# Load order, queues and input transposes at the start of a long-convolution kernel with a two-row router

## The chip, the cores and the metric

The kernel runs on one core of a Trainium2 chip. The core has TensorE (matrix products, into PSUM), VectorE, ScalarE, GpSimd and SyncE, each with its own strictly ordered list of instructions; they meet through semaphores. Transfers are started from an engine's list (here SyncE's and ScalarE's) and carried out by 16 DMA engines. The metric is the device time of one execution in microseconds (us); less is better.

## The reference, cut to what matters

```python
x = A_u                                           # (1, 2048, 512) bf16
g = sigmoid((x * gate_w).sum(-1, keepdims=True))  # a gate for each row
a = A_ref(x, ...)     # a long convolution along the rows, one kernel K for each of 512 channels:
                      #   dt = exp(log_dt); P = exp(dt*(A_re + 1j*A_im) * l)    for 2048 lags l
                      #   K  = real(sum_n C * P * dt*B)                          n = 128 states
                      #   a  = irfft(rfft(x) * rfft(K)) + x * Dskip
b = B_ref(B_x, ...)   # r = x @ w_r; the two rows with the largest r go through
                      #   silu(x_sel @ w_gate) * (x_sel @ w_up) @ w_down, times sigmoid(r),
                      #   and are added to x at their places
return g * a + (1 - g) * b
```

The kernel takes its rows, and those of the second branch, from the one input A_u.

## The kernel before, in words

**Data.** U holds the 2048 x 512 input in SBUF: 16 row blocks of 128 rows, arranged so that within each 256 rows the even and the odd ones are apart. XT holds the input transposed (512 channels on partitions, in four groups of 128). PRM holds the six parameter tables (A_re, A_im, C_re, C_im, B_re, B_im), each 512 x 128 in memory and 128 x 512 in SBUF, so each is transposed by the DMA that loads it. LDT is log_dt spread over all partitions. F is the 2 MB matrix of the forward transform; NG, two buffers, is a part of its negative, loaded in four pieces. CB and CF hold constants (the identity among them), WL the two weight vectors of gate and router. WG, WU and WD are the weights of the two-row feed-forward.

**Stages.** (1) Parameters: DTB = exp(LDT), AL = DTB * A_re, B16 = the phase step from DTB * A_im, WW from B and C. (2) For each half h of the channels, tables of exp(AL * lag) (`exps1`, `exps2`: 32 and 16 activations) times sines and cosines of B16 * lag (`trig`, called by `tab1` and `tab2`). (3) `routing`: logits of gate and router (`lg`, 64 products of XT with WL), two rounds of a maximum over all rows (`gmax`: VectorE reduces, TensorE transposes, VectorE reduces, twice a round), gathering the two rows, the feed-forward (`ffn1` for gate and up, Silu, `dn`), and one-hot rows OHR to put the result back. (4) `forward`: the transform of the input, 16 blocks of 16 matmuls (two more in the second half of the rows), each block evicted from PSUM to X. (5) `xupd`: the branch's rows are added to U, and U is scaled by 1 - g. (6) `kgen` and `kspec`: the convolution kernel and its transform for each half, from the tables and a 3.5 MB matrix KP. (7) `products` and `inverse` for each half, and the stores.

**Order.** Each operation is put into a list by `P.op` with an engine, what it reads and writes, an estimated cost and a priority. `schedule()` then plays a model of the engines and queues: it places, again and again, the operation that can start earliest in the model, and among equals the one with the longest way to the end plus its priority. `P.boost = 100` stands while `routing()` is written down. That play fixes the order on each engine; at run time each engine goes through its list and waits by semaphores. `EV` gives an eviction to ScalarE or VectorE, whichever would be done first in the model; `SCL` does the same for the angle operations. DMA issues are placed in the same way: those with `eng=SP` on SyncE's list, those with `eng=ACT` on ScalarE's. `tset` numbers the phases of ScalarE's function tables (exponential in even, sine, tanh and Silu in odd): no operation of a later phase is placed before all of an earlier one are. Phase 0 is `exps1(0)` and `exps2(0)`; 1 is `tab1(0)`, half of `tab2(0)` and the router's tanh and Silu; 2 is `exps1(1)`; 3 the rest of `tab2(0)` and `tab1(1)`; 4 is `exps2(1)`; 5 is `tab2(1)`.

**The loads at the start.** On SyncE's list: LDT; the transposing loads of A_re and A_im; four transposing loads of A_u into XT, one for each 128 channels; the transposing loads of C_re, C_im, B_re and B_im; CF, WG, WU, two pieces of NG, Dskip. On ScalarE's list: the two halves of U, F, CB, and the two loads of WL.

`lg` reads XT by rows in U's even and odd order, so with a step of two:

```python
last = h.matmul(b(0, 128, tb * 2, (1, 2)),
                XT(0, 128, db * L + 1024 * j + 256 * st + par, (2, 128)),
                WL(0, 128, db * 2, (1, 2)), start=(db == 0), stop=(db == 3))
```

In the profile the helpers `TT`, `TS`, `AC`, `EV`, `SCL`, `CP`, `STT` and `DMA` record their operations under their own lines: L387 is a VectorE operation on two tensors (`TT`), L391 and L392 one with a scalar (`TS`), L394 `STT`, L396 `CP`, L398 an activation (`AC`), L402 an eviction (`EV`), L406 an angle operation (`SCL`), L409 a load or store. L242 is a table load of ScalarE, L463 and L475 the transposing loads of parameters and input, L598 `lg`, L612 a reduction and L617 a transpose of `gmax`, L639 the gather, L648 the one-hot transposes, L659 `ffn1`, L670 `dn`, L693 and L695 `forward`, L713 to L732 `kgen`, L754 `kspec`, L804 `inverse`, L830 and L831 `xupd`.

Of the kernel before, what the change touches and what calls it, by code (L numbers as in the profile page):

```python
# [27 lines left out]
def dr(a, off, *dims):  # L28
    return bass.AP(a.tensor, off, [[s, c] for (s, c) in dims])
# [225 lines left out]
L, D, NS, NF = 2048, 512, 128, 1792  # L255
# [71 lines left out]
def bass_gated_mix__ssm_conv_s4__moe_arch_mod__prompt_kernel(nc, A_u, A_A_re, A_A_im, A_B_re, A_B_im, A_C_re, A_C_im, A_log_dt, A_Dskip,  # L327
# [24 lines left out]
    with ExitStack() as es:  # L352
# [55 lines left out]
        def DMA(pairs, rd, wr, nbytes, eng=SP, **k):  # L408
            return P.op(eng, lambda h: [h.dma_start(o, i) for o, i in pairs], rd, wr, cost=0.5 * len(pairs), n=len(pairs), nbytes=nbytes, dma=True, **k)  # L409
# [42 lines left out]
        def misc(bf=False):  # L452
            mc[0] += 1
            return (misb if bf else mis)[mc[0] % 2]
# [6 lines left out]
        DMA([(LDT(0, 128, 0, (1, D)), dr(A_log_dt, 0, (0, 128), (1, D)))], [], [LDT], 131072, prio=2e5)  # L461
        for i in (1, 0, 2, 3, 4, 5):
            P.op(SP, lambda h, i=i: h.dma_start_transpose(PRM(0, 128, i * D, (1, D)), dr(prm[i], 0, (128, D), (1, 128))), [], [(PRM, i)], cost=1.25, nbytes=131072, prio=(1.9e5 if i < 2 else 1.2e5) - 1e3 * i)  # L463
        for j in range(2):
            DMA([(U(0, 128, j * 8 * D, (2 * D, 4), (1, 2 * D)), dr(A_u, 1024 * j * D, (2 * D, 128), (256 * D, 4), (1, 2 * D)))], [], [(U, t) for t in range(8 * j, 8 * j + 8)], 1048576, eng=ACT, prio=2e5)
        DMA([(F(0, 128, 0, (1, 8192)), f_c[:, :])], [], [F], 2097152, eng=ACT, prio=1.9e5)
        DMA([(CB(0, 128, 0, (1, 384)), cb_c[:, :])], [], [CB], 98304, eng=ACT, prio=1.8e5)
        def ld_w(h):
            with nc.allow_non_contiguous_dma(reason="tiny weight vectors"):
                a = h.dma_start(WL(0, 128, 0, (2, 4), (1, 1)), dr(gate_w, 0, (1, 128), (128, 4), (1, 1)))  # L470
                b = h.dma_start(WL(0, 128, 1, (2, 4), (1, 1)), dr(B_w_r, 0, (1, 128), (128, 4), (1, 1)))
            return [a, b]
        P.op(ACT, ld_w, [], [WL], cost=1.0, n=2, nbytes=100000, dma=True, prio=1.7e5)
        for db in range(4):
            P.op(SP, lambda h, db=db: h.dma_start_transpose(XT(0, 128, db * L, (1, L)), dr(A_u, db * 128, (D, L), (1, 128))), [], [(XT, db)], cost=4.2, nbytes=524288, prio=1.5e5)  # L475
        DMA([(CF(0, 128, 0, (1, 160)), cf_c[:, :])], [], [CF], 81920, prio=1.1e5)
        DMA([(WG(0, 128, 0, (NF, 4), (1, NF)), dr(B_w_gate, 0, (NF, 128), (128 * NF, 4), (1, NF)))], [], [WG], 1835008, prio=1.0e5)
        DMA([(WU(0, 128, 0, (NF, 4), (1, NF)), dr(B_w_up, 0, (NF, 128), (128 * NF, 4), (1, NF)))], [], [WU], 1835008, prio=0.9e5)
        DMA([(DSK(0, 1, 0, (1, D)), dr(A_Dskip, 0, (D, 1), (1, D)))], [], [DSK], 1024)

        IDN = lambda *a: CB(0, 128, *a)

# [104 lines left out]


        def routing():
            b = misc()  # L590
            def lg(h):
                last = None
                for j in range(2):
                    for st in range(4):
                        for par in range(2):
                            tb = j * 8 + st * 2 + par
                            for db in range(4):
                                last = h.matmul(b(0, 128, tb * 2, (1, 2)), XT(0, 128, db * L + 1024 * j + 256 * st + par, (2, 128)), WL(0, 128, db * 2, (1, 2)), start=(db == 0), stop=(db == 3))  # L598
# [78 lines left out]
        def forward():  # L677
            np_ = [0]
            for ft in range(4):
                ng = NG[ft % 2]  # L680
                DMA([(ng(0, 128, 0, (128, 8), (1, 128)), bass.AP(fn_c.tensor, fn_c.offset + ft * 128, [[4096, 128], [512, 8], [1, 128]]))], [], [ng], 262144)
# [225 lines left out]
```

## Time and profile before

| | us |
|---|---|
| median of three runs | 247.95 (247.47 to 248.18) |
| the profiled execution | 246.49 |
| its span, first to last instruction | 244.7 |
| TensorE busy in it | 172.5 (70%) |
| VectorE busy in it | 170.4 (70%) |
| ScalarE busy in it | 146.9 (60%) |

The busy times are those of one profiled execution. The page cuts the span into 40 slices and gives the busy share of each engine in each slice as a digit (9 is 90% or more); the timeline lists instructions by their start, with the wait before them and what ended it in square brackets; a line that begins with SPq or ACTq is the issue of a transfer on that engine's list. TensorE's matmuls overlap, so that its busy time is not its time at full rate. The mean granted TensorE clock over the span was 0.927 of full speed.

### The profile page before, as it was taken

How to read it: one execution, taken by the hardware profiler on the slowest of the kernel's cores; microseconds unless marked ns; L12 is line 12 of the kernel's file. 1: busy time of each engine (PE TensorE's matmuls, PEld its weight loads, DVE VectorE, ACT ScalarE, POOL GpSimd, SP SyncE). 2: the span in 40 equal slices, each digit the busy share in tenths (PEclk: the TensorE clock that was granted, in tenths of full speed). 3: DMA queues.
4: the chain of work that ended last, by engine and by line, in shares of the span. 5: the costliest groups of instructions: out<-in, count | busy, mean ns of one | idle time of the engine just before them, and what ended most of it. 6: DMA issues, size and time to landing. Idle time of an engine off the chain costs nothing.

```text
span 244.7 us, 3534 instructions
## 1 busy us (share of the span) xinstructions
PE 172.5 (70%) x1426; PEld 103.4 (42%) x1426; DVE 170.4 (70%) x279; ACT 146.9 (60%) x278; POOL 0.2 (0%) x4
## 2 busy tenths in 40 slices
PE   0000030349999999999899506999898999973993
PEld 0000020147444444445555201366665667862882
DVE  0002223899995039989850299969999999999872
ACT  0330999349989899549876999656664454404000
POOL 0000000000000000000000000000000000000000
PEclk9999999999999999999999755589997999996798
DMA  4999959903600101000006800000027000001144
GB/s 143 324 253 161 205 120 360 330 3 87 217 0 3 43 0 43 3 0 0 4 0 220 378 5 0 1 0 3 0 46 300 3 0 0 3 0 48 38 132 128
DMA packets 25953, 22.03 MB, mean 90 GB/s; under 512 B 17233, under 2 KB 23506, under 8 KB 25554
## 3 DMA queue, kind: packets, MB, share of 16 engines
q1 hardware_dynamic: 23538, 17.52, 25.9%
q10 hardware_dynamic: 2400, 4.30, 6.7%
q8 instruction: 11, 0.18, 0.3%
q14 instruction: 4, 0.03, 0.0%
HBM read 16.83 MB, written 2.10 MB: 77 GB/s over the span
## 4 chain that ended last, share of the span: by engine, by line
PE 43%; DVE 24%; ACT 20%; DMA 8%; issue 3%; SPq 1%; DVEq 0%; ACTq 0%
DVE AR L387 21%; PE ps L693 19%; ACT AR L398 13%; DMA AR<-in_A_A_im_dram 8%; PE ps L804 7%; PE ps L754 6%; ACT AR L402 3%; PE ps L831 3%; PE ps L830 2%; ACT AR L406 2%; DVE AR L391 2%; PE ps L659 1%; PE ps L670 1%; PE ps L695 1%; ACT L242 1%
## 5 line engine op out<-in xcount | busy, mean ns | idle before, releaser
L387 DVE TENSOR_TENSOR AR<-AR 128x1024 bf16<-128x1024 bf16 (+5 forms) x182 | 136.8, 804 | 34.7 <-DMA AR<-in_A_A_re_dram 11.6
L398 ACT ACTIVATE AR<-AR 128x256 bf16<-128x256 f32 (+2 forms) x132 | 64.7, 560 | 15.4 <-DVE AR L391 4.8
L402 ACT ACTIVATE AR<-ps 128x1024 bf16<-128x1024 f32 (+6 forms) x58 | 45.5, 806 | 30.7 <-PE ps L754 17.7
L693 PE MATMUL ps<-AR 128*128 128x512 bf16 x256 | 59.6, 385 | 0.0
L693 PEld LDWEIGHTS ps<-AR 128*128 128x128 bf16 x256 | 25.1, 99 | 30.5 <-issue 1.9
L804 PE MATMUL ps<-AR 128*128 128x256 bf16 x256 | 30.8, 286 | 5.5 <-ACT AR L398 5.5
L754 PE MATMUL ps<-AR 128*128 128x256 bf16 x224 | 33.3, 286 | 0.7 <-ACT AR L402 0.7
L804 PEld LDWEIGHTS ps<-AR 128*128 128x128 bf16 x256 | 26.1, 103 | 10.0 <-DVE AR L387 5.8
L754 PEld LDWEIGHTS ps<-AR 128*128 128x128 bf16 x224 | 21.9, 101 | 12.2 <-issue 1.5
L398 ACT ACTIVATE AR<-ps,AR 128x512 bf16<-128x512 f32 (+1 forms) x32 | 16.6, 586 | 15.5 <-DVE AR L387 10.4
L598 PE MATMUL ps<-AR 128*128 128x2 bf16 x64 | 1.8, 165 | 32.2 <-DMA AR<-in_A_u_dram 32.2
L406 ACT ACTIVATE AR<-AR 128x256 int32<-128x256 f32 x50 | 17.6, 405 | 10.9 <-DVE AR L387 10.7
L391 DVE TENSOR_SCALAR AR<-AR 128x1024 int32<-128x1024 int32 (+5 forms) x32 | 16.2, 524 | 8.4 <-ACT AR L398 8.0
L402 DVE CAST AR<-ps 128x1024 bf16<-128x1024 f32 (+3 forms) x6 | 5.1, 865 | 22.5 <-PE ps L695 15.4
L830 PE MATMUL ps<-AR 128*128 128x512 bf16 x16 | 8.1, 509 | 11.0 <-ACT AR L398 11.0
L598 PEld LDWEIGHTS ps<-AR 128*128 128x128 bf16 x64 | 1.8, 104 | 32.1 <-issue 32.1
L713 PE MATMUL ps<-AR 128*128 128x84 bf16 x256 | 11.8, 201 | 2.4 <-ACT AR L402 2.4
L713 PEld LDWEIGHTS ps<-AR 128*128 128x128 bf16 x256 | 10.6, 98 | 4.5 <-ACT AR L402 3.2
L617 PE MATMUL ps<-AR 128*128 128x128 f32 x4 | 1.9, 475 | 12.8 <-DVE AR L391 12.8
L394 DVE SCALAR_TENSOR_TENSOR AR<-ps,AR 128x256 bf16<-128x256 f32 x16 | 6.9, 479 | 4.1 <-PE ps L804 4.1
L726 PE MATMUL ps<-AR 128*32 128x128 bf16 (+1 forms) x96 | 8.5, 381 | 0.0
L830 PEld LDWEIGHTS ps<-AR 128*128 128x128 bf16 x16 | 1.6, 100 | 15.7 <-ACT AR L398 14.6
(32 smaller groups left out, 62.1 us busy)
## 6 DMA issues: line engine op xcount, KB each, us to landing
AR<-c_ksp SPq DMA_DIRECT2D x1, 3584.0 KB, 12.5
AR<-in_A_u_dram ACTq DMA_DIRECT2D x2, 1024.0 KB, 12.0
AR<-c_fwd ACTq DMA_DIRECT2D x1, 2048.0 KB, 20.0
AR<-c_inv SPq DMA_DIRECT2D x1, 2048.0 KB, 7.9
out_dram<-AR SPq DMA_DIRECT2D x16, 128.0 KB, 2.2
AR<-in_B_w_gate_dram SPq DMA_DIRECT2D x1, 1792.0 KB, 7.1
AR<-in_B_w_up_dram SPq DMA_DIRECT2D x1, 1792.0 KB, 11.2
AR<-in_B_w_down_dram SPq DMA_DIRECT2D x1, 1792.0 KB, 7.9
```

The costliest lines, as they stand in the source:

```text
L387: return P.op(DVE, lambda h: h.tensor_tensor(out=o, in0=a, in1=b, op=op), rd, wr, cost=tt_cost(o, a, b), **k)
L391: return P.op(DVE, lambda h: h.tensor_scalar(out=o, in0=a, scalar1=s1, scalar2=None, op0=op0), rd, wr, cost=c, **k)
L398: return P.op(ACT, lambda h: h.activation(out=o, in_=a, func=func, scale=scale, bias=bias), rd, wr, cost=0.185 + nel(o) * 0.833e-3 + (0.09 ...
L402: return P.op((ACT, DVE), (lambda h: h.activation(out=o, in_=a, func=ACTF.Copy), lambda h: h.tensor_copy(o, a)), rd, wr, cost=(0.185 + n * ...
L406: return P.op((ACT, DVE), (lambda h: h.activation(out=o, in_=a, func=ACTF.Copy, scale=c), lambda h: h.tensor_scalar(out=o, in0=a, scalar1= ...
L693: last = h.matmul(o, w, U(0, 128, (blk * 8 + st * 2 + par) * D, (1, D)), start=(par + st == 0), stop=(par * 4 + st == 7 and blk == 0))
L713: last = hh.matmul(pb(0, 128, (g - b0) * 84, (1, 84)), TP[h][1 - part](0, 128, g * 128, (1, 128)), TQ[h][1 - part](0, 128, g * 84, (1, 84) ...
L726: last = hh.matmul(pb(32 * g, 32, c4, (256, njg), (4, 64)), lw, KA[h](0, 128, c4 + 4 * (8 * bk + g), (16, njg), (84, 64)), start=True, sto ...
L754: last = hh.matmul(pb(0, 128, n * 256, (1, 256)), KP(0, np_, u * 2048 + tau * 128, (1, 128)), KC[h](0, np_, jg * 256, (1, 256)), start=(k ...
L804: last = hh.matmul(pb(0, 128, e * 256, (1, 256)), G(0, 128, ((par * 2 + part) * 4 + ft) * 512 + (2 * t2 + e) * 128, (1, 128)), X(0, 128, h ...
L830: h.matmul(pb(0, 128, c0, (1, D)), IDN(0, (1, 128)), U(0, 128, tb * D, (1, D)), start=True, stop=False)
L831: return h.matmul(pb(0, 128, c0, (1, D)), OHR(0, 2, tb * 128, (1, 128)), ZB(0, 2, D, (1, D)), start=False, stop=True)
```

## The change

The first loads are put in a fixed order, by falling priorities. LDT, CB and WL go on ScalarE's list, and nothing else. SyncE's list begins with A_re and A_im, then U in two halves, the other four parameter tables, F, CF, two pieces of NG, WG, WU and Dskip. The four transposing loads of A_u are gone; in their place the router begins with eight steps on TensorE, each of which transposes two row blocks of U (eight 128 x 128 transposes into one PSUM buffer), and an eviction of 1024 elements to XT. XT is then in U's order, and `lg` reads it without a step. The first two pieces of NG are no longer loaded from `forward`, and the last two get a higher priority. The planner's estimate of WL's size falls from 100000 to 20000 bytes.

```diff
-        DMA([(LDT(...), dr(A_log_dt, ...))], [], [LDT], 131072, prio=2e5)
-        for i in (1, 0, 2, 3, 4, 5):
-            P.op(SP, lambda h, i=i: h.dma_start_transpose(PRM(0, 128, i * D, (1, D)), dr(prm[i], ...)), [], [(PRM, i)], cost=1.25, nbytes=131072, prio=(1.9e5 if i < 2 else 1.2e5) - 1e3 * i)
-        for j in range(2):
-            DMA([(U(...), dr(A_u, 1024 * j * D, ...))], [], [(U, t) for t in range(8 * j, 8 * j + 8)], 1048576, eng=ACT, prio=2e5)
-        DMA([(F(...), f_c[:, :])], [], [F], 2097152, eng=ACT, prio=1.9e5)
-        DMA([(CB(...), cb_c[:, :])], [], [CB], 98304, eng=ACT, prio=1.8e5)
...
-        P.op(ACT, ld_w, [], [WL], cost=1.0, n=2, nbytes=100000, dma=True, prio=1.7e5)
-        for db in range(4):
-            P.op(SP, lambda h, db=db: h.dma_start_transpose(XT(0, 128, db * L, (1, L)), dr(A_u, db * 128, (D, L), (1, 128))), [], [(XT, db)], cost=4.2, nbytes=524288, prio=1.5e5)
...
+        dp = [3e5]
+        def DQ(pairs, rd, wr, nbytes, **k):
+            dp[0] -= 1e3
+            return DMA(pairs, rd, wr, nbytes, prio=dp[0], **k)
+        def prm_t(i):
+            dp[0] -= 1e3
+            P.op(SP, lambda h: h.dma_start_transpose(PRM(0, 128, i * D, (1, D)), dr(prm[i], ...)), [], [(PRM, i)], cost=1.25, nbytes=131072, prio=dp[0])
+        DQ([(LDT(...), dr(A_log_dt, ...))], [], [LDT], 131072, eng=ACT)
+        DQ([(CB(...), cb_c[:, :])], [], [CB], 98304, eng=ACT)
+        P.op(ACT, ld_w, [], [WL], cost=1.0, n=2, nbytes=20000, dma=True, prio=2.5e5)
+        prm_t(0)
+        prm_t(1)
+        for j in range(2):
+            DQ([(U(...), dr(A_u, 1024 * j * D, ...))], [], [(U, t) for t in range(8 * j, 8 * j + 8)], 1048576)
+        for i in range(2, 6):
+            prm_t(i)
+        DQ([(F(...), f_c[:, :])], [], [F], 2097152)
+        DQ([(CF(...), cf_c[:, :])], [], [CF], 81920)
+        for ft in range(2):
+            DQ([(NG[ft](...), ngsrc(ft))], [], [NG[ft]], 262144)
+        DQ([(WG(...), dr(B_w_gate, ...))], [], [WG], 1835008)
+        DQ([(WU(...), dr(B_w_up, ...))], [], [WU], 1835008)
+        DQ([(DSK(...), dr(A_Dskip, ...))], [], [DSK], 1024)
...
         def routing():
+            for q in range(8):
+                bb = misc(True)
+                def tr(h, q=q, bb=bb):
+                    last = None
+                    for t_ in range(2):
+                        for db in range(4):
+                            last = h.transpose(bb(0, 128, db * 256 + t_ * 128, (1, 128)), U(0, 128, (2 * q + t_) * D + db * 128, (1, 128)), IDN(0, (1, 128)))
+                    return last
+                P.op(PE, tr, [(U, 2 * q), (U, 2 * q + 1), CB], [bb.buf], cost=0.7)
+                EV(XT(0, 128, q * 256, (L, 4), (1, 256)), bb(0, 128, 0, (256, 4), (1, 256)), [bb.buf], [(XT, q)])
...
-                                last = h.matmul(b(...), XT(0, 128, db * L + 1024 * j + 256 * st + par, (2, 128)), WL(...), ...)
+                                last = h.matmul(b(...), XT(0, 128, db * L + tb * 128, (1, 128)), WL(...), ...)
...
-                DMA([(ng(...), ...)], [], [ng], 262144)
+                if ft > 1:
+                    DMA([(ng(...), ngsrc(ft))], [], [ng], 262144, prio=2e5)
```

More of the change, by code (lines that the diff above doesn't have):

```diff
@@ L460, in bass_gated_mix__ssm_conv_s4__moe_arch_mod__prompt_kernel, with ngsrc @@
         prm = [A_A_re, A_A_im, A_C_re, A_C_im, A_B_re, A_B_im]
-        DMA([(LDT(0, 128, 0, (1, D)), dr(A_log_dt, 0, (0, 128), (1, D)))], [], [LDT], 131072, prio=2e5)
-        for i in (1, 0, 2, 3, 4, 5):
-            P.op(SP, lambda h, i=i: h.dma_start_transpose(PRM(0, 128, i * D, (1, D)), dr(prm[i], 0, (128, D), (1, 128))), [], [(PRM, i)], cost=1.25, nbytes=131072, prio=(1.9e5 if i < 2 else 1.2e5) - 1e3 * i)
-        for j in range(2):
-            DMA([(U(0, 128, j * 8 * D, (2 * D, 4), (1, 2 * D)), dr(A_u, 1024 * j * D, (2 * D, 128), (256 * D, 4), (1, 2 * D)))], [], [(U, t) for t in range(8 * j, 8 * j + 8)], 1048576, eng=ACT, prio=2e5)
-        DMA([(F(0, 128, 0, (1, 8192)), f_c[:, :])], [], [F], 2097152, eng=ACT, prio=1.9e5)
-        DMA([(CB(0, 128, 0, (1, 384)), cb_c[:, :])], [], [CB], 98304, eng=ACT, prio=1.8e5)
+        def ngsrc(ft):
+            return bass.AP(fn_c.tensor, fn_c.offset + ft * 128, [[4096, 128], [512, 8], [1, 128]])
         def ld_w(h):
@@ L597, in lg @@
                             for db in range(4):
[L598 removed]
+                                last = h.matmul(b(0, 128, tb * 2, (1, 2)), XT(0, 128, db * L + tb * 128, (1, 128)), WL(0, 128, db * 2, (1, 2)), start=(db == 0), stop=(db == 3))
                 return last
```

16 lines of the change are left out of this document (11 added, 5 removed).

## The prediction, as it stood before the run

> **What bounds the kernel now.** I read the page first: the slices of the span.
>
> ```profile
> span 244.7 us, 3534 instructions
> PE   0000030349999999999899506999898999973993
> DVE  0002223899995039989850299969999999999872
> ACT  0330999349989899549876999656664454404000
> GB/s 143 324 253 161 205 120 360 330 3 87 217 0 3 43 0 43 3 0 0 4 0 220 378 5 0 1 0 3 0 46 300 3 0 0 3 0 48 38 132 128
> ```
>
> A slice is 6.1 us. TensorE does almost nothing for eight slices, ScalarE idles in most of the first four, and VectorE is full only from the seventh on; over the last ten VectorE is full. No engine bounds the whole. So I cut the span where ScalarE changes its function table: exponentials of half 0; sines of half 0 with the router; exponentials of half 1; sines; exponentials; sines; then the products and the last inverse. Windows view (busy time, count in brackets):
>
> ```profile
> 0.00:38.90 38.90, 1.85 (x64) 1.79 (x64) 6.39 (x12) 17.75 (x54) 0.20 (x4) 1.00 1.00 204
> 38.90:72.06 33.16, 21.47 (x249) 12.30 (x250) 29.36 (x69) 24.44 (x42) 0.00 (x0) 1.00 0.50 167
> 72.06:87.97 15.91, 15.91 (x75) 6.97 (x74) 4.58 (x8) 15.04 (x38) 0.00 (x0) 1.00 0.08 18
> 87.97:124.14 36.17, 35.18 (x233) 17.61 (x232) 32.90 (x55) 28.95 (x44) 0.00 (x0) 1.00 0.04 8
> 124.14:138.24 14.10, 13.65 (x126) 6.79 (x124) 3.13 (x5) 10.03 (x24) 0.00 (x0) 0.88 0.53 207
> 138.24:164.77 26.53, 15.93 (x59) 6.65 (x60) 21.87 (x40) 21.41 (x32) 0.00 (x0) 0.61 0.07 29
> 164.77:223.50 58.73, 51.85 (x499) 37.54 (x496) 58.04 (x66) 26.72 (x40) 0.00 (x0) 0.96 0.10 37
> ```
>
> The columns are stretch, length, TensorE, its weight loads, VectorE, ScalarE, GpSimd, clock, DMA share, GB/s. Stage 1 (38.9 us) has 17.75 us of ScalarE work and all 16 DMA engines busy (share 1.00). From stage 2 on ScalarE or VectorE is nearly full, with TensorE beside them. The next views say what stage 1 waits for: ScalarE's timeline, the DMA issues (last number: us from issue to landing), and the queues.
>
> ```profile
> 0.73 1.00 ACTq L409 DMA_DIRECT2D AR<-in_A_u_dram  x2
> 1.76 1.48 ACTq L409 DMA_DIRECT2D AR<-c_fwd  x1
> 6.56 1.28 ACT L398 ACT_TABLE_LOAD   x1 [6.56 <-issue]
> 12.35 1.95 ACT L398 ACTIVATE AR<-AR 128x256 bf16<-128x256 f32 x6 [3.87 <-DVE AR L387]
> 24.99 0.72 ACT L406 ACTIVATE AR<-AR 128x256 int32<-128x256 f32 x2 [10.70 <-DVE AR L387]
> 26.54 12.34 ACT L398 ACTIVATE AR<-AR 128x256 bf16<-128x256 f32 x40
> 38.90 1.28 ACT L242 ACT_TABLE_LOAD   x1
> 66.46 1.00 ACT L402 ACTIVATE AR<-ps 128x1024 bf16<-128x1024 f32 x1
> ```
>
> ```profile
> AR<-in_A_A_re_dram SPq DMA_TRANSPOSE x1, 10.3
> AR<-in_A_A_im_dram SPq DMA_TRANSPOSE x1, 19.4
> AR<-in_A_C_re_dram SPq DMA_TRANSPOSE x1, 2.8
> AR<-in_A_log_dt_dram SPq DMA_DIRECT2D x1, 128.0 KB, 5.0
> AR<-c_bf ACTq DMA_DIRECT2D x1, 96.0 KB, 19.0
> 1.20 1.90 SPq L463 DMA_TRANSPOSE AR<-in_A_A_re_dram  x1
> 4.66 25.11 SPq L475 DMA_TRANSPOSE AR<-in_A_u_dram  x4
> 36.68 7.35 SPq L409 DMA_DIRECT2D AR<-c_fwdn  x2
> ```
>
> The six parameter tables are alike in size; C_re, alone in the queues, lands in 2.8 us, A_re beside the 4 MB of U and F in 10.3, A_im in 19.4. The exponentials need A_re (AL); the angle operations, put on ScalarE after six exponentials, need A_im (B16), and the strict order makes everything behind them wait 10.70 us. The sum is made against the profiled execution, 246.49 us around a span of 244.7; the median of the three runs is 247.95, 1.46 more.
>
> **The change, part by part: stage 1.** ScalarE's queue loses the issues of U and F (1.00 + 1.48 us) and gains that of LDT (A_re's issue at 1.20 follows it, 0.47 after the queues start at 0.73): 6.56 becomes 4.5. Table load 1.28, first exponential 0.63 and VectorE's AL 0.69 follow, so the exponentials start near 7.1 instead of 12.35, if A_re is there: issued at 0.73, it lands at 3.5 with C_re's 2.8, at 11.0 with its own 10.3. I take 2.8, since U is now issued behind it on the same queue and only the small loads run on the other. A_im, issued near 2.7 (A_re's issue took 1.90), lands at 5.5 by C_re's row, 13 by A_re's; B16 comes about 2.4 us of VectorE work later, at 9.4 after AL, or at 15.4. After six exponentials ScalarE is at 9.1: it waits 0.3 us, or 6.3. I take 0.3.
>
> The Trainium skill, page "DMA: Bandwidth & Descriptors", section "Queues, rings and completion order", says that one ring is consumed in order and that each DMA engine takes turns between the queues packet by packet. A_re's 10.3 us beside the other queue's 4 MB agree; by it U on the same ring cannot delay A_re, and the sum would be the one I take.
>
> ScalarE has then 48 exponentials at 12.34/40 = 0.31 (14.8 us), three angle operations at 0.31, and its share of the eight new XT evictions, 1024 elements each, at 1.00 by the row of 66.46: between 0 and 8 of them (VectorE idles here, so 4 is the middle). 7.1 + 14.8 + 0.9 + 4.0 = 26.8 instead of 38.9, **12.1 us** gained; ends 22.8 (16 gained) and, with eight evictions on ScalarE, 30.8 (8 gained), or 37 with A_im late as well.
>
> The 64 TensorE transposes and the reads of U fall into time in which TensorE is idle: eight transposes take 1.01 us below, 8.1 us in all, from about 9 us (U is behind 0.26 MB of transposes; 2.1 MB at 324 GB/s are 6.5 us) to 18. If that cover went, the router would start 8.1 us later, at 26, still ahead of 29.8, when the last input transpose is issued now (4.66 + 25.11). CB, which the transposes need, and WL, which the first logits need, have only LDT ahead of them in their queue: I take LDT's 5.0 us; CB's own 19.0 would put them at 20 to 23, and the router still ahead of 29.8.
>
> What leaves SP's queue are four input transposes, 25.11 us of issue. F goes behind U and four parameter tables: 5.2 MB in all, at the mean of the first five slices (217 GB/s) 24 us, at the best slice (360) 15; I take 22, and NG0 a little later instead of about 44. The gate and up weights come behind them, sooner than now, where they follow all ten transposes. The second NG's issue sat in a full queue for most of 7.35 us; the same stall may now meet it, but behind it wait only DSK, the later NG and the down weights, which nothing needs for 15 us more.
>
> **Stage 2, the sines.** The first forward block needs F and NG0 and ran at 59.4, behind the router's first feed-forward product; it can now run from 23. The views of the chain and of TensorE:
>
> ```profile
> 51.99 1.01 PE L648 MATMUL ps<-AR 128*2 128x128 bf16 x8
> 59.47 10.04 PE ps L693 x40
> 76.82 1.73 PE ps L693 x8
> 78.77 8.63 PE ps L693 x40
> ```
>
> The evictions of forward are what its blocks cost the other engines. A block is two groups of 1.73 us, 3.46 us, and needs one eviction of 1 us. In stage 2 there will be about eight instead of two: six more, three on each engine. Against that, the router's maxima can run under the exponentials, where VectorE idles. Now they stand in VectorE's full stretch:
>
> ```profile
> L391 DVE TENSOR_SCALAR AR<-AR 128x128 f32<-128x128 f32 (+3 forms) x8 | 2.7, 340 | 3.8 <-ACT AR L398 3.6
> L612 DVE TENSOR_REDUCE AR<-ps 128x1 f32<-128x128 f32 x4 | 1.2, 290 | 0.7 <-PE ps L617 0.7
> L394 DVE SCALAR_TENSOR_TENSOR AR<-AR 128x16 f32<-128x16 f32 (+1 forms) x4 | 0.9, 216 | 0.1
> L396 DVE CAST AR<-AR 128x16 f32<-128x16 bf16 (+2 forms) x6 | 0.8, 169 | 0.1
> L612 DVE TENSOR_REDUCE AR<-AR 128x1 f32<-128x16 f32 x4 | 0.7, 170 | 0.1
> ```
>
> That is some 6 us (2.7 less about 1.1 for the tables' own two, then 1.2 + 0.9 + 0.8 + 0.7, and waits of 0.7). VectorE has 29.36 - 6 + 3.6 = 27, ScalarE 24.44 + 3 = 27.5; with a us for waits, stage 2 takes 28.5 instead of 33.16: **4.7 us**. Ends: nothing, where the router stays in the way; 8.7, ScalarE's own 24.44.
>
> **Stages 3 to 5.** Stage 3 is ScalarE's exponentials with forward evictions among them, as now: nothing. In stage 4 VectorE has 32.90 of 36.17; forward, from 23 on, 16 blocks of 3.46 and some 12 us of router between (TensorE's 21.47 us in stage 2 less the 12.6 from 59.47 on, and the down projection), ends near 90 instead of in stage 5, so a few of its evictions leave: **2 us**, ends 0 and 5.3 (down to VectorE's 32.90 less two evictions). In stage 5 ScalarE has 10.03 of 14.10 us:
>
> ```profile
> ACT AR L402 <- PE ps L726: 2.1, 1, 2.1
> ACT AR L398 <- PE ps L695: 1.7, 1, 1.7
> PE ps L830 <- ACT AR L398: 11.0, 2, 10.7
> ```
>
> The first two are waits for TensorE, which does the last forward blocks between the kernel-table products; with forward gone they go: **4 us**, ends 0 and 5.
>
> **Stages 6 to the end.** VectorE has 58.04 of 58.73 us after 164.77, and the stage before takes it 21.87 of 26.53. I take nothing gained; ends are the 4.7 us of that idle time, gained if all of it goes, or lost if it doubles with TensorE's low clock. That was 0.61 in the stage, with a wait of 10.7 us (the last row above). By the Trainium skill, "TensorE: Matmul & The Clock Gate", Part 1, idle windows of about 3.4 us halve the clock and as much activity restores it. The start of forward agrees (the first 40 matmuls took 10.04, the next 40 8.63); the 0.61 over 26.5 us lasts longer than that rule says. By it a shorter wait would give back some of the 4.7 us, and the sum would be up to that much lower, which is part of the good end below; I take the row.
>
> Sum: 12.1 + 4.7 + 2 + 4 = 22.8. 246.49 - 22.8 = 223.7, and 1.46 more for the median: **225 us**.
>
> **The rivals.** *Only the start is kept.* The order of each engine is written by the planner with its own durations; if forward's evictions and the router fill what stage 2 frees, and TensorE still ends forward late, only stage 1's gain counts, with most evictions on ScalarE: 8 to 12 us, 236 to 240. For it speaks that ScalarE is already 74% busy in stage 2; against it, that TensorE's idle first 59 us are real room.
>
> *Slower: the router between forward blocks.* The exponentials of half 1 cannot pass the Silu on ScalarE, and that needs the router's nine TensorE steps (four maxima, gather, two transposes, two products). Now they run with nothing between. With forward ready at 23, each may sit behind a block. At 3.46 us a step Silu comes at 22 + 9 x 3.46 = 53, just inside stage 2's end of 55. If blocks wait in turn for evictions that stand behind sines, a step becomes 7 us: Silu at 85, 13 us after the present 72, less the 6 of stages 4 and 5: 255. It decides from (72 - 22 + 6)/9 = 6.2 us a step. Against it: evictions came every 3.5 us in stage 3 already.
>
> *Everything at its good end:* 16 + 8.7 + 5.3 + 5 + 4.7 = 39.7, so 208.
>
> **How the numbers follow.** The forecast (219 to 234) has 0.53, only the start 0.22, the good end 0.11, slower 0.10, and 0.04 that the pieces cancel within 0.3% (about what three runs can tell). Faster 0.86, same 0.04, slower 0.10. Leaving out the slower rival and the tail of the good end gives 211 to 241.
>
> **What would show it.** Right: A_im lands before 7 us, no wait of ScalarE over 2 us before the second table load, which comes at 23 to 31; no input transposes in SP's queue; the first forward block at 19 to 27; VectorE's maxima before the sines; the third table load near 55. Wrong: parameter tables that still take 10 us, ScalarE waiting for XT's PSUM or for U among the exponentials, Silu after 65, or new waits for TensorE in the sine stages.

## The result

| | median, us | all runs | ratio to before, 95% interval |
|---|---|---|---|
| before, beside the runs of after | 248.06 | 247.47 to 248.38 | |
| after | 225.45 | 224.77 to 227.63 | 0.9106 (0.9039 to 0.9173) |

The change takes 22.6 us off the median; 225 was predicted, 211 to 241 the range. The profiled execution of after took 227.63 us (span 225.8), the slowest of its four runs; its span is 18.9 us below the 244.7 of before, where the prediction's terms add up to 22.8. So 3.9 us of the agreement in the median are not in the trace that is read here: that the median fell on the forecast is in part luck.

### The profile page after: what moved, and what is told of

It is laid out like the page before. It is cut to its first block, busy times and chain, and to the rows that moved or that the text cites. A ratio compares the mean times of both kernels' runs of the same rounds, so it can differ in the third digit from the quotient of the medians.

```text
span 225.8 us, 3655 instructions
## 1 busy us (share of the span) xinstructions
PE 182.8 (81%) x1480; PEld 111.4 (49%) x1490; DVE 173.1 (77%) x283; ACT 151.0 (67%) x282; POOL 0.2 (0%) x4
## 4 chain that ended last, share of the span: by engine, by line
PE 49%; DVE 23%; ACT 21%; issue 3%; DMA 2%; SPq 1%; DVEq 0%; ACTq 0%
DVE AR L387 19%; PE ps L715 18%; ACT AR L398 12%; PE ps L776 8%; PE ps L826 7%; ACT AR L402 6%; PE ps L735 3%; DVE AR L391 3%; PE ps L853 2%; ACT AR L406 2%; PE ps L852 2%; PE ps L748 2%; DMA AR<-in_A_A_im_dram 2%; PE ps L691 1%; PE ps L680 1%
## 5 line engine op out<-in xcount | busy, mean ns | idle before, releaser
L387 DVE TENSOR_TENSOR AR<-AR 128x1024 bf16<-128x1024 bf16 (+6 forms) x182 | 136.9, 804 | 9.3 <-DMA AR<-in_A_A_re_dram 5.8
L402 ACT ACTIVATE AR<-ps 128x1024 bf16<-128x1024 f32 (+7 forms) x62 | 50.2, 827 | 33.9 <-PE ps L776 17.3
L398 ACT ACTIVATE AR<-AR 128x256 bf16<-128x256 f32 (+4 forms) x132 | 65.1, 559 | 3.3 <-DVE AR L387 1.5
L715 PE MATMUL ps<-AR 128*128 128x512 bf16 x248 | 62.9, 408 | 2.0 <-ACT AR L402 1.1
L715 PEld LDWEIGHTS ps<-AR 128*128 128x128 bf16 x256 | 26.4, 104 | 35.5 <-issue 8.6
L826 PEld LDWEIGHTS ps<-AR 128*128 128x128 bf16 x256 | 26.1, 102 | 9.8 <-DVE AR L387 5.7
L776 PEld LDWEIGHTS ps<-AR 128*128 128x128 bf16 x224 | 21.7, 100 | 12.0 <-issue 1.5
L398 ACT ACTIVATE AR<-ps,AR 128x512 bf16<-128x512 f32 (+1 forms) x32 | 16.6, 584 | 15.5 <-DVE AR L387 10.3
L607 PE MATMUL ps<-AR 128*128 128x128 bf16 x64 | 7.5, 311 | 11.6 <-DMA AR<-in_A_u_dram 9.5
L735 PE MATMUL ps<-AR 128*128 128x84 bf16 x256 | 13.3, 214 | 3.2 <-ACT AR L402 3.2
L852 PE MATMUL ps<-AR 128*128 128x512 bf16 x14 | 7.2, 512 | 10.2 <-ACT AR L398 10.2
L735 PEld LDWEIGHTS ps<-AR 128*128 128x128 bf16 x256 | 11.8, 106 | 5.1 <-ACT AR L402 4.3
L607 PEld LDWEIGHTS ps<-AR 128*128 128x128 bf16 x64 | 6.5, 145 | 12.4 <-DMA AR<-in_A_u_dram 9.5
L396 DVE CAST AR<-ps 128x16 bf16<-128x16 f32 (+3 forms) x6 | 1.5, 256 | 13.7 <-PE ps L691 12.9
L402 DVE CAST AR<-ps 128x1024 bf16<-128x1024 f32 (+4 forms) x7 | 5.7, 837 | 7.0 <-PE ps L748 4.4
L852 PEld LDWEIGHTS ps<-AR 128*128 128x128 bf16 x16 | 1.6, 99 | 15.0 <-ACT AR L398 13.1
L853 PE MATMUL ps<-AR 2*128 2x512 bf16 x16 | 7.9, 495 | 0.7 <-DVE AR L402 0.5
## 6 DMA issues: line engine op xcount, KB each, us to landing
AR<-in_B_w_up_dram SPq DMA_DIRECT2D x1, 1792.0 KB, 12.6
```

The source lines that it names most:

```text
L387: return P.op(DVE, lambda h: h.tensor_tensor(out=o, in0=a, in1=b, op=op), rd, wr, cost=tt_cost(o, a, b), **k)
L398: return P.op(ACT, lambda h: h.activation(out=o, in_=a, func=func, scale=scale, bias=bias), rd, wr, cost=0.185 + nel(o) * 0.833e-3 + (0.09 ...
L402: return P.op((ACT, DVE), (lambda h: h.activation(out=o, in_=a, func=ACTF.Copy), lambda h: h.tensor_copy(o, a)), rd, wr, cost=(0.185 + n * ...
L607: last = h.transpose(bb(0, 128, db * 256 + t_ * 128, (1, 128)), U(0, 128, (2 * q + t_) * D + db * 128, (1, 128)), IDN(0, (1, 128)))
L715: last = h.matmul(o, w, U(0, 128, (blk * 8 + st * 2 + par) * D, (1, D)), start=(par + st == 0), stop=(par * 4 + st == 7 and blk == 0))
L735: last = hh.matmul(pb(0, 128, (g - b0) * 84, (1, 84)), TP[h][1 - part](0, 128, g * 128, (1, 128)), TQ[h][1 - part](0, 128, g * 84, (1, 84) ...
```

## The profile after

Each fence below shows the lines that a reading rests on; lines between them may be left out. The page's slices, 5.6 us each now:

```profile
span 225.8 us, 3655 instructions
PE   0366798959999999997893089998898999945993
DVE  0729369998600599999823999799999999999863
ACT  3799999998689896399969995656834455205000
PEclk9999589967699999999667555999969999995899
GB/s 95 363 312 319 405 192 1 36 13 3 302 23 49 0 0 0 0 3 1 79 381 193 0 1 0 3 0 0 3 345 29 0 3 0 0 0 73 23 162 117
```

ScalarE is full from the third slice (before: from the fifth), TensorE works from the second (before: little until the ninth), and the loads fill the first six slices. The first digit 5 in the clock row stands where the first forward block runs.

The windows view of after, cut at the same table loads of ScalarE as before (length, TensorE, weight loads, VectorE, ScalarE, GpSimd, clock, DMA share, GB/s); the last row is the last stage of sines, and the span goes on to 225.8:

```profile
0.00:28.25 28.25, 13.77 (x139) 9.99 (x141) 12.91 (x29) 22.50 (x59) 0.20 (x4) 0.90 0.99 299
28.25:56.97 28.72, 24.80 (x262) 13.69 (x262) 25.55 (x54) 27.00 (x46) 0.00 (x0) 0.86 0.14 48
56.97:74.41 17.44, 17.15 (x83) 7.29 (x83) 4.18 (x9) 14.24 (x36) 0.00 (x0) 0.91 0.40 121
74.41:108.39 33.98, 31.95 (x219) 16.39 (x221) 31.04 (x51) 27.07 (x42) 0.00 (x0) 0.99 0.00 1
108.39:119.96 11.57, 10.88 (x106) 6.36 (x105) 5.40 (x10) 9.47 (x24) 0.00 (x0) 0.73 0.70 276
119.96:146.08 26.12, 15.93 (x61) 6.52 (x61) 21.87 (x41) 21.40 (x32) 0.00 (x0) 0.61 0.05 20
```

Against the rows of before: stage 1 38.90 to 28.25 (-10.65), stage 2 33.16 to 28.72 (-4.44), stage 3 15.91 to 17.44 (+1.53), stage 4 36.17 to 33.98 (-2.19), stage 5 14.10 to 11.57 (-2.53), and 106.46 to 105.84 (-0.62) for all that follows. That is the 18.9 us.

Stage 1 in ScalarE's timeline of after, and the landing times (last number, us from issue):

```profile
6.52 1.95 ACT L398 ACTIVATE AR<-AR 128x256 bf16<-128x256 f32 x6 [1.51 <-DVE AR L387]
9.17 0.72 ACT L406 ACTIVATE AR<-AR 128x256 int32<-128x256 f32 x2 [0.70 <-DVE AR L387]
11.63 1.00 ACT L402 ACTIVATE AR<-ps 128x1024 bf16<-128x1024 bf16 x1
18.35 1.94 ACT L402 ACTIVATE AR<-ps 128x1024 bf16<-128x1024 bf16 x2 [0.21 <-PE ps L607]
```

```profile
AR<-in_A_A_re_dram SPq DMA_TRANSPOSE x1, 5.0
AR<-in_A_A_im_dram SPq DMA_TRANSPOSE x1, 4.8
AR<-c_bf ACTq DMA_DIRECT2D x1, 96.0 KB, 4.3
```

A_im needs 4.8 us instead of 19.4, A_re 5.0 instead of 10.3, CB 4.3 instead of 19.0. The wait of 10.70 us before the angle operations is 0.70. Five evictions of XT (L402, the first and the last two shown) stand among the exponentials.

TensorE's timeline, the forward blocks (L715) between the router's steps:

```profile
24.23 5.96 PE L715 MATMUL ps<-AR 128*128 128x512 bf16 x15 [0.22 <-issue]
30.13 3.62 PE L715 MATMUL ps<-AR 128*128 128x512 bf16 x16
48.91 5.56 PE L715 MATMUL ps<-AR 128*128 128x512 bf16 x15 [0.33 <-issue]
57.52 6.41 PE L715 MATMUL ps<-AR 128*128 128x512 bf16 x23 [0.24 <-issue]
103.07 0.38 PE L717 MATMUL ps<-AR 128*128 128x512 bf16 x1
```

Forward starts at 24.23 instead of 59.4, but ends only at 103: the blocks behind the router's steps at 24.23, 48.91 and 57.52 run slowly (the last section looks at this).

## The experiments

Two questions: which part of the change brings stage 1's gain, and what limits the time after it. All medians beside their own runs of before (247.6 to 248.2); stage 1 ends with ScalarE's first change to sines, stage 2 with the change back. Three kernels keep every order of after, or change it only by hand: the queue of U and F, the fewer products and the last one. For the others the planner wrote each engine's order anew, so their differences hold the edit and the new order together.

| kernel | median, us | ratio, 95% interval | stage 1 ends | stage 2 ends |
|---|---|---|---|---|
| after | 225.45 | 0.9039 to 0.9173 | 28.25 | 56.97 |
| XT by transposing loads, new order and queues | 235.71 | 0.9449 to 0.9644 | 22.75 | 64.60 |
| before with TensorE transposes | 254.19 | 1.0078 to 1.0414 | 46.32 | 84.53 |
| U and F on the other queue | 236.5 | 0.9426 to 0.9678 | 39.12 | 67.73 |
| XT evicted by VectorE | 225.9 | 0.9071 to 0.9212 | 22.79 | 56.70 |
| forward late | 234.12 | 0.9425 to 0.948 | 27.99 | 57.17 |
| both of the last two | 235.11 | 0.9472 to 0.9514 | 23.02 | 50.25 |
| 64 forward products fewer | 222.91 | 0.8965 to 0.9035 | 27.95 | 55.74 |
| XT by transposing loads behind NG | 245.08 | 0.9851 to 0.9945 | 22.79 | 70.15 |
| Silu in a later phase | 228.23 | 0.9147 to 0.9211 | 28.18 | 55.58 |
| VectorE evictions and late Silu | 229.65 | 0.9215 to 0.9281 | 23.00 | 56.42 |
| transposing loads behind NG, late Silu | 242.05 | 0.9727 to 0.9806 | 22.79 | 71.23 |
| first maximum ahead on VectorE | 223.3 | 0.8964 to 0.9033 | 22.87 | 53.47 |

**Only the queue of U and F.** Every order of after is kept; three issues move.

```diff
+        mv = [...]   # the two loads of U, the load of F, taken from SyncE's finished list
+        for k_, o in enumerate(mv):
+            P.order[SP].remove(o)
+            P.order[ACT].insert(1 + k_, o)   # behind LDT, ahead of CB and WL
+            o.eng = ACT
```

> The changed kernel with every engine's order kept, but the three issues of U and F moved from SP's queue to ScalarE's, behind LDT and ahead of CB and WL. Theory A: A_re lands at about 10 us and A_im at 15 to 20, the three angle operations behind the sixth exponential wait for it, the second table load comes 8 to 14 us later than 28.25, and the time is 233 to 240 us. Theory B (the queue does not matter once the input's transposing loads are gone): A_im lands before 8 us and the time is 224 to 228 us; only ScalarE's own issues of about 2.5 us come on top.

236.5 us, in Theory A's range; the profiled execution took 238.27, the slowest of four (the fastest took 234.49). ScalarE's timeline, TensorE's, and the landing times of this kernel:

```profile
18.12 0.72 ACT L406 ACTIVATE AR<-AR 128x256 int32<-128x256 f32 x2 [5.80 <-DVE AR L387]
22.47 1.02 ACT L402 ACTIVATE AR<-ps 128x1024 bf16<-128x1024 bf16 x1 [1.80 <-PE ps L607]
```

```profile
21.43 1.86 PE L607 MATMUL ps<-AR 128*128 128x128 bf16 x16 [21.43 <-DMA AR<-c_bf]
```

```profile
AR<-in_A_A_re_dram SPq DMA_TRANSPOSE x1, 8.8
AR<-in_A_A_im_dram SPq DMA_TRANSPOSE x1, 13.7
AR<-c_bf ACTq DMA_DIRECT2D x1, 96.0 KB, 18.1
```

The table load at 39.12 is 10.87 us later than in after, and the stages behind it are those of after within 0.12 us each (28.61, 17.41, 33.98, 11.56): the whole 11 us is stage 1. Of it, 3.85 us are the later start of the exponentials (10.37 instead of 6.52: ScalarE's table load stands behind the issues, and A_re comes late too), 5.1 the wait for A_im (5.80 instead of 0.70), and most of the rest the wait for the transposes behind CB. A_im beside 4 MB of the other queue takes 13.7 us instead of 4.8, and CB, now behind that 4 MB in its own queue, 18.1 instead of 4.3. The Trainium skill, "DMA: Bandwidth & Descriptors", section "Queues, rings and completion order", has both rules, one ring in order and the DMA engines taking turns between queues; these rows agree with both.

**Transposes on TensorE alone, in the old order and queues.**

```diff
 # before
-        for db in range(4):
-            P.op(SP, ... dma_start_transpose(XT ...
         def routing():
+            for q in range(8):
+                ...            # the eight steps and evictions of the change, lg in their order
```

> The kernel before with one edit: XT is made by TensorE and evictions, the four transposing loads of A_u are gone; order and queues of all other loads as before (U, F, CB, WL on ScalarE's queue). Theory A: A_im still lands late (15 to 19 us, beside 4 MB from the other queue), CB and WL too, ScalarE's second table load comes at 36 to 42 us, and the time is 238 to 247 us. Theory B: A_im lands before 9 us, the second table load comes before 32 and the time is 225 to 231 us.

254.19 us: slower than before (0.8 to 4.1%), and slower than either theory's range. TensorE's and ScalarE's timelines:

```profile
22.44 1.89 PE L594 MATMUL ps<-AR 128*128 128x128 bf16 x16 [22.44 <-DMA AR<-c_bf]
38.71 1.94 PE L594 MATMUL ps<-AR 128*128 128x128 bf16 x16 [14.38 <-ACT AR L402]
```

```profile
25.09 0.72 ACT L406 ACTIVATE AR<-AR 128x256 int32<-128x256 f32 x2 [10.78 <-DVE AR L387]
41.93 2.85 ACT L402 ACTIVATE AR<-ps 128x1024 bf16<-128x1024 bf16 x3 [0.21 <-PE ps L594]
```

The identity in CB lands 19.4 us after its issue, A_im is as late as before (19.8 us), and the planner put seven evictions on ScalarE at the end of the exponentials, where TensorE waits 14.38 us for them; they account for most of the 7.4 us by which stage 1 is longer. Taking 2 MB of transposing loads out of the queues does not by itself bring A_re and A_im sooner.

**The new order and queues alone.** XT comes by its four transposing loads, behind U and ahead of the other parameters and F.

```diff
 # after
-            for q in range(8):  ...   # transposes and evictions
+        for db in range(4):           # behind U
+            dp[0] -= 1e3
+            P.op(SP, ... dma_start_transpose(XT ...
```

> The new load order and queues, but XT still comes by four transposing loads of A_u on SP's queue, placed behind U and ahead of the other four parameter tables; no TensorE transposes, no XT evictions. Theory A (the early parameter tables make the gain, because U and F no longer share the DMA engines with them from another queue): A_im lands by 7 us as in the changed kernel, ScalarE's second table load comes at 23 to 24 (five evictions of about 1 us fewer than at 28.25), forward starts near 40 because F stands behind 2 MB of transposes, and the time is 229 to 234 us. Theory B (the transposing loads of the input are what held everything up, and TensorE's transposes are the gain): the table load comes after 33 and the time is 238 us or more.

235.71 us, between the two ranges. Stage 1 is short (22.75, with no eviction on ScalarE), as Theory A has it: the gain of stage 1 needs no transposes on TensorE. But VectorE idles behind the transposing loads, and the router with it. VectorE's timeline, then TensorE's:

```profile
25.04 1.23 DVE L387 TENSOR_TENSOR AR<-AR 128x1024 f32<-128x1024 bf16 x1 [15.08 <-DMA AR<-in_A_B_re_dram]
```

```profile
35.75 0.48 PE L631 MATMUL ps<-AR 128*128 128x128 f32 x1 [11.46 <-DVE AR L391]
36.02 5.37 PE L708 MATMUL ps<-AR 128*128 128x512 bf16 x16
```

The four issues take 15.26 us of SyncE's list; B_re behind them lands at 25, VectorE's products with it stand ahead of the first maximum (L631 is `gmax` here), and stage 2 takes 41.85 us.

**The same loads at another place: behind NG, ahead of WG.**

```diff
+        for db in range(4):           # behind the two pieces of NG
+            P.op(SP, ... dma_start_transpose(XT ...
```

> As the run with XT by transposing loads in the new order, but these loads stand behind the parameter tables, F, CF and the first two pieces of NG instead of ahead of four tables and F. If the 10 us that run lost to the changed kernel came from what stood behind the transposing loads (VectorE's strict order waited 15 us for B_re, forward for F), VectorE now waits less than 3 us for B_re and the time is 224 to 229 us: TensorE's transposes are then worth nothing by themselves. If it came from the router starting late: logits at 30 us or later and 232 to 237 us.

245.08 us, beyond both ranges. No parameter waits for these loads now, but the logits stand behind the first forward blocks. TensorE's and VectorE's timelines:

```profile
21.86 10.50 PE L708 MATMUL ps<-AR 128*128 128x512 bf16 x40 [21.86 <-DMA AR<-c_fwdn]
38.24 1.74 PE L612 MATMUL ps<-AR 128*128 128x2 bf16 x64
39.84 3.61 PE L708 MATMUL ps<-AR 128*128 128x512 bf16 x16
```

```profile
40.02 0.17 DVE L396 CAST AR<-ps 128x16 bf16<-128x16 f32 x1 [10.76 <-PE ps L612]
```

VectorE's strict order has the casts of the logits ahead of the sine tables, so it idles 10.76 us at that place; stage 2 takes 47.36 us and Silu comes at 69.91. Here the router runs between forward blocks, as in the prediction's slower rival, but not at its price: the nine steps from the logits to Silu took 3.5 us each, and what differs from after is that they begin at 38.24 and not at 20.34. This points to the early logits as the gain of the transposes on TensorE; they also spare SyncE's list the 12.6 to 15.3 us of the transposing issues. Only these two places were tried, each with the order that the planner made for it.

To see whether Silu, the last operation of that chain in ScalarE's phase, is what holds the stage, it was moved to the next sine phase:

```diff
-  AC(..., ACTF.Silu, [(HB, 0)], [(HB, 2)], tset=1)     # and the second tanh
+  AC(..., ACTF.Silu, [(HB, 0)], [(HB, 2)], tset=3)
```

> The same move on top of the run with XT by transposing loads behind NG (245.08 us, sine stage from 22.8 to 70.2 us, Silu at 69.9). Theory E (TensorE's input transposes pay because they let the router start early, and the router's Silu gates the exponentials of half 1): without the gate the sine stage ends at 50 to 58 us and the time falls to 228 to 236 us. Rival (what costs is the late router as such, its result in the update of the rows, or forward's later blocks): the time stays above 240 us.

242.05 us, stage 2 ends at 71.23, the rival's case: Silu does not hold it. VectorE idles for the logits as before (10.75 us), and at the end ScalarE waits 2.98 us for a forward block; which of the two sets the end is not separated.

**Where evictions of XT go.** All eight on VectorE:

```diff
-                EV(XT(...), bb(...), [bb.buf], [(XT, q)])
+                P.op(DVE, lambda h, ...: h.tensor_copy(XT(...), bb(...)), [bb.buf], [(XT, q)], cost=0.7)
```

> The changed kernel with all eight XT evictions on VectorE (0.69 us each by its own three), none on ScalarE. ScalarE's second table load comes at 23 to 24.5 instead of 28.25. Theory A (ScalarE's phases are the chain from start to end, so what stage 1 gains reaches the end): 220 to 222.5 us. Theory C (from about 47 us on TensorE's forward blocks are the chain, as the chain view of the changed kernel shows them, and their start is set by F): 224 to 226 us.

225.9 us, Theory C's range, but not for its reason. Stage 1 is 5.46 us shorter and stage 2 takes nearly all of it back (it ends 0.27 us sooner). TensorE's, VectorE's and ScalarE's timelines:

```profile
26.22 0.47 PE L638 MATMUL ps<-AR 128*128 128x128 f32 x1 [6.45 <-DVE AR L391]
26.49 6.14 PE L715 MATMUL ps<-AR 128*128 128x512 bf16 x16
```

```profile
24.33 0.38 DVE L392 TENSOR_SCALAR AR<-AR 128x16 bf16<-128x16 f32 x2 [1.97 <-ACT AR L398]
```

```profile
32.67 1.02 ACT L402 ACTIVATE AR<-ps 128x1024 bf16<-128x1024 f32 x1 [3.07 <-PE ps L715]
```

Forward stands behind the transpose of the first maximum, not behind F, and that waits 6.45 us for VectorE, where the gate's operations (L392; they need ScalarE's first tanh, behind its table load) are ahead. In after the planner had put the first maximum in front of them. The last experiment below tests this.

**What forward's early start is worth.** Its blocks wait for the router's first feed-forward products (gate and up); then the same with VectorE's evictions.

```diff
-                        rd = [F, CB, ng] + [(U, ...)]
+                        rd = [F, CB, ng, (HB, 0), (HB, 1)] + [(U, ...)]
```

> The changed kernel, but every forward block waits for the router's two feed-forward products, as the planner's order had it in the kernel before; loads and XT as changed. My prediction's step (an early forward takes its evictions and its waits out of the later sine stages, 6 us): 230 to 233 us. Rival D (TensorE ends forward at about the same moment either way: in the changed kernel it runs from 24 to 103 us with router steps between, of which some 6 us are matmuls at half clock behind router steps; without interleaving it would run from about 40 to 103): within 1.5 us of the changed kernel's 225.45, and TensorE's last forward block ends at 101 to 105 us.

> Both edits: XT evictions all on VectorE, and forward behind the router's feed-forward products. If in the run with the evictions alone the early exponentials were lost because the router's maxima and forward held the sine stage, the sine stage now ends some 4 us sooner than at 56.97: 220 to 223 us. If TensorE's forward work after that sets the end, no change: 224 to 227 us.

TensorE's timeline of the first kernel, where forward begins:

```profile
48.74 9.89 PE L715 MATMUL ps<-AR 128*128 128x512 bf16 x32 [8.53 <-DVE AR L396]
```

234.12 and 235.11 us, in none of the four ranges: the early start is worth 8.7 us (the prediction's 2 and 4 of stages 4 and 5 make 6). Stages 2 and 4 of the second kernel in the windows view:

```profile
23.02:50.25 27.23, 9.99 (x199) 7.46 (x200) 24.75 (x57) 23.32 (x43) 0.00 (x0) 0.50 0.52 190
68.22:113.22 45.00, 42.97 (x304) 21.93 (x302) 32.89 (x56) 33.24 (x49) 0.00 (x0) 1.00 0.05 13
```

Stage 2 ends 6.7 us sooner than in after, without any gain: TensorE, busy for 9.99 of 27.23 us at a clock of 0.50 in stage 2, is full in stage 4, which is 11.0 us longer. Both halves have to come early. The rival of the first expectation (no change) is wrong, and its first range (230 to 233) 1.1 us too low; both halves of the other are wrong.

**Is TensorE the bound then?** A quarter of forward's products left out, so that the result is not the transform; orders kept.

```diff
-                                    for st in range(4):
+                                    for st in (range(0, 4, 3) if ft in (1, 2) else range(4)):
```

> The changed kernel with half the matmuls of forward's second and third quarter left out (64 of 256; the result is then not the transform), all orders kept: 13.8 us less TensorE work between about 49 and 88 us. Theory C (TensorE is the chain from 47 to 98 us): 8 to 14 us less, 211 to 217 us. Theory A (ScalarE's table phases and VectorE's tables are the chain, TensorE runs beside them): no more than 3 us less, 222 to 226 us.

222.91 us, in Theory A's range: 13.8 us less TensorE work (64 products at 1.73/8) brings 2.5. Stage 3 is 3.5 us shorter (13.94; ScalarE's waits for forward are gone), stage 4 1.9. So TensorE's work alone does not set the time; less work for ScalarE or VectorE was not tried.

**Silu in after.** The edit of the late phase, on after and on the kernel with VectorE's evictions:

> The changed kernel with the router's Silu and its second tanh moved from ScalarE's sine phase to the next one with the same table, so that the exponentials of half 1 no longer wait for the router. Theory E (in the changed kernel the sine stage is held by the router's chain, whose TensorE steps stand behind forward blocks; Silu ran at 56.11, the stage ended at 56.97): with 27.0 of its 28.72 us busy ScalarE can give back at most 1.7 us here: 223.5 to 225.5 us. Rival (the router's result is needed later on and comes late): 226 us or more.

> The same move of Silu and second tanh, on top of the run with all XT evictions on VectorE, in which the exponentials ended 5.5 us sooner and the sine stage at the same 56.7, 0.25 us after Silu. Theory E: without that gate the sine stage ends 3 to 5 us sooner, at 52 to 54 us, and the time is 220 to 223 us. Theory F (TensorE's forward blocks and kernel-table products set the end of the later sine stage, whatever the exponentials do): the stage ends sooner, the time stays at 224 to 226.5 us.

228.23 and 229.65: neither is faster than the kernel without the move (225.45 and 225.9), the first is in its rival's range and the second in neither of its ranges. In the first, stage 2 is 1.3 us shorter, stage 4 2.5 longer, stage 5 2.0 shorter, and what follows 1.3 longer (107.1 us): the time is only moved. In the second, stage 2 still ends at 56.42, now behind a forward block's eviction, for which ScalarE waits 1.97 us until 54.47.

**The first maximum ahead on VectorE.** XT evicted by VectorE, and five operations moved in its finished order.

```diff
+        od = P.order[DVE]
+        at = ...   # the first operation that needs the gate's tanh
+        mv = [...] # scaling, maximum, candidates, maximum, scaling of the router's first round
+        for o in mv: od.remove(o)
+        od[at:at] = mv
```

> All eight evictions of XT are on VectorE, as in the earlier experiment whose exponentials ended at 22.8 us and which was still no faster (225.9, third table load at 56.7); and VectorE's five operations for the first maximum (scaling, maximum, candidates, maximum, scaling) now stand ahead of the gate's four, which wait for ScalarE's first tanh behind the table load. Every other order is unchanged. Theory A: the 5.5 us were lost because the first maximum stood behind the gate's wait: its TensorE transpose waited 6.45 us, the first forward block stood behind that and started at 26.49, and ScalarE waited 3.07 us for its eviction. Then the first forward block starts near 23, ScalarE's wait of 3.07 us goes, the third table load comes at 53 to 54.5 and the total is 221.5 to 224. Theory B: in the stage of sines VectorE is the bound (from 33 us on it never waited) and TensorE's forward sets the end later: the forward blocks start near 23 as well, but the third table load stays at 55.5 or later and the total at 225 to 227.

223.3 us, in Theory A's range, and the fastest complete kernel. TensorE's and ScalarE's timelines:

```profile
22.92 0.47 PE L638 MATMUL ps<-AR 128*128 128x128 f32 x1 [2.96 <-DVE AR L391]
23.19 6.22 PE L715 MATMUL ps<-AR 128*128 128x512 bf16 x16
```

```profile
29.59 1.00 ACT L402 ACTIVATE AR<-ps 128x1024 bf16<-128x1024 f32 x1
```

Forward starts 3.30 us sooner than with VectorE's evictions alone, ScalarE's wait of 3.07 us is gone, and the table load comes 3.23 us sooner. The later stages keep their lengths (15.88, 33.98 and 11.53), so it goes through to the end: the median is 2.6 us below that kernel's, and 2.2 below after's; the intervals (0.8964 to 0.9033 and 0.9039 to 0.9173) just miss each other. So 3.2 of the 5.2 us that stage 2 had taken back lay in the order of a few short operations; where the other 2 lie stays open.

## Why the prediction was right, step by step

- **Stage 1, 12.1 predicted, 10.65 measured.** The mechanism is shown: with only U and F back on the other queue all of it goes. Its start was right (exponentials at 6.52, 7.1 predicted; A_im landed at 6.8, under 7; the stall 0.70 instead of 0.3), though A_re, with U behind it and small loads on the other queue, took 5.0 us and not the 2.8 of C_re's row. It ended 1.45 us later than forecast: 0.6 sooner at the start, 0.4 more of the stall, 1.0 for a fifth eviction on ScalarE (four were taken), 0.4 of waits for TensorE's transposes, and 0.25 unaccounted.
- **Cover of the transposes and loads.** CB in 4.3 us (5.0 taken); transposes from 9.47 to 19.2 (9 to 18); forward at 24.23 (23). The cover is real, and the transposes on TensorE are worth having: with the transposing loads at either place that was tried the time is 10.3 us longer (in front) or 19.6 (behind NG).
- **Stage 2, 4.7 and 4.44.** The length was right, part of the reason wrong. VectorE's 25.55 us are near the 27, but only the first of the four maxima ran under the exponentials; VectorE then waited 4.59 us for the gate's tanh, and the other three ended among the sines. Forward needed five evictions here and not eight, all on ScalarE, which is busy 27.00 us (27.5 taken) and waits 0.9 us for a block, which is new.
- **Stage 3, 0 and +1.53.** This step failed: "forward evictions among them, as now" left out that ScalarE would wait for the blocks. First before, then after, in this stage:

```profile
ACT AR L402 <- PE ps L693: 0.8, 2, 0.6
```

```profile
ACT AR L402 <- PE ps L715: 2.0, 1, 2.0
ACT AR L402 <- PE ps L717: 1.1, 2, 0.7
```

ScalarE waits 2.3 us more and has 0.8 us less to do (an eviction fewer). With 64 forward products fewer these waits are gone and the stage takes 13.94 us.

- **Stage 4, 2 and 2.19.** Right in size: VectorE has 31.04 us to do instead of 32.90, one forward eviction (1.2 us) fewer among it. But forward ends at 103 and not at 90, so that ScalarE still waits 5.5 us for its blocks (6.0 before): the blocks were priced at 3.46 us each, where those behind router steps took 5.6 to 6.4 for 15 to 23 products, and ScalarE's evictions and the steps between took their time.
- **Stage 5, 4 and 2.53.** The term took two waits as forward's, 2.1 and 1.7 us. Only the second was: it is gone. The first, for the kernel-table products (L726, now L748), remains, though forward ended 5 us before this stage (and is 3.2 us with 64 forward products fewer):

```profile
ACT AR L402 <- PE ps L748: 2.0, 1, 2.0
```

- **Stages 6 to the end, 0 and -0.62.** As taken: VectorE's bound and the stage's clock of 0.61 are those of before.
- **The rivals.** "Only the start is kept" (236 to 240) did not come in after; forward late gives it nearly (234.12). The slower rival's price per step was not reached (logits 20.34, Silu 56.11: nine steps in 35.8 us, 4.0 each, where 6.2 decides). The good end did not come: with VectorE's evictions stage 1 gave its 16 us (22.79), and stage 2 took 5.2 of them back.

The terms that were too large (stages 1, 3, 5) add up to 4.5 us against the profiled span; the median of after lies lower than its profiled run by 2.2, while that of before lay 1.6 above, and this difference brought the forecast to its mark. That is luck; the mechanism of the largest term, stage 1, is not.

## What to carry to other kernels

Put the few small loads that the first work needs at the head of their queues and keep bulk transfers out of every other queue until they have landed: here that alone was worth 11 us. A transpose moved from the queues to an idle engine paid here only with its constant and its input early; in the old order and queues it cost 6 us. And when a stage gets shorter but its end doesn't move, look in the strict orders for a short operation behind a longer wait: five moved operations made the stage end 3.2 us sooner.

## What was not expected of the hardware

The granted clock falls behind the router's steps (thin products, mostly with waits between), although TensorE is not idle for long. The windows view of after, from the first maximum to the end of the second block, and around the block at 48.91:

```profile
20.00:24.23 4.23, 2.23 (x66) 2.03 (x68) 3.50 (x10) 4.23 (x15) 0.00 (x0) 0.80 1.15 331
24.23:30.00 5.77, 5.77 (x15) 2.12 (x15) 1.04 (x7) 5.74 (x17) 0.00 (x0) 0.55 1.03 407
42.80:48.91 6.11, 3.31 (x81) 2.93 (x81) 6.08 (x12) 5.74 (x9) 0.00 (x0) 0.80 0.21 46
48.91:54.30 5.39, 5.39 (x15) 2.05 (x15) 5.39 (x9) 4.74 (x8) 0.00 (x0) 0.59 0.00 0
```

With TensorE busy for about half of the 4.23 and 6.11 us before them, the next blocks run at 0.55 and 0.59, 15 products in 5.96 and 5.56 us where the block at 30.13 does 16 in 3.62. About 2 us are lost each time. If the clock is either full or half, 0.55 over 5.77 us and 0.59 over 5.39 are, as an estimate, 5.2 and 4.4 us at half clock. The Trainium skill, "TensorE: Matmul & The Clock Gate", Part 1, says that a freely running window of some 3.4 us of activity restores the clock; 4.4 to 5.2 us lie between one and two such windows, so the trace agrees.

Thin products alone need not do it: with the transposing loads behind NG the 64 products at 38.24 follow a block without a wait, and the next block does 16 in 3.61 us. Nor are the waits all of it: in after the block at 57.52 stands behind 2.97 us of thin products and a wait of 0.24, and takes 6.41 us for 23. What exactly lowers the clock stays open. And the clock column does not show every slow stretch: in "forward late" the 32 products at 48.74, behind 8.53 us without work, took 9.89 us, where 40 later ones take 8.80, and the column says 1.00 throughout.

The same eviction of 128 x 1024 bf16 from PSUM takes 0.69 us on VectorE and 1.00 on ScalarE (the row of 11.63 above). VectorE's timeline of after:

```profile
14.62 0.69 DVE L402 COPY AR<-ps 128x1024 bf16<-128x1024 bf16 x1 [2.53 <-PE ps L607]
```

From f32 it takes 1.00 on ScalarE and 1.22 on VectorE. The planner's model prices both by the latter pair (1.04 and 1.22 by `EV`), which may be why five of the eight went to ScalarE, the engine that bounds stage 1.
